# Moving one output store of the last row tile to the ScalarE queue

## Chip, cores, metric

The kernel runs on one core of one Trainium2 chip. The metric is device time in microseconds (us), the median of the runs of one kernel. Besides it the text uses the *span*, the time from the first to the last instruction in a profiled run, and the *tail*, the part of the span after the last VectorE copy has ended. Both are read from the trace, in nanoseconds (ns) where that matters.

## The reference, cut to what matters

Two linear-attention blocks A and B run on the same input `x` (2048 rows, 640 columns, bf16), and a gate for each row mixes their outputs:

```python
g = _sigmoid((x * gate_w).sum(-1, keepdims=True))
a = _A_ref(x, A_wqkv, A_wo)
b = _B_ref(x, B_wqkv, B_wo)
return g * a + (1 - g) * b          # 1 x 2048 x 640, bf16
```

Only the last step concerns us: the output leaves the core in 16 row tiles of 128 rows by 640 columns.

## The kernel before

The kernel lists its operations with their dependencies, and a small scheduler fixes the order on each engine before the program is built. The last row tile is computed in two column pieces, so that the first can be copied and stored while TensorE works on the second:

```python
def o_post(t, ps, lo, hi, eng):
    os_, bo = Buf("os", "os"), Buf("ob")
    w = hi - lo
    if eng == "ADD":
        ...                                     # tiles 0 to 12: add to an earlier partial sum
    elif eng == "DVE":
        op("DVE", lambda e: e.tensor_copy(OST[:, os_.slot, 0:w], psw(ps, w)), ...)
    else:
        op("ACT", lambda e: e.activation(OST[:, os_.slot, 0:w], psw(ps, w), ACT.Copy), ...)
    final.append(dma("SP", "out%d_%d" % (t, lo),
                     outd[128 * t : 128 * t + 128, lo:hi],
                     lambda: OST[:, os_.slot, 0:w], 128 * w * 2, ins=[os_], outs=[bo]))

def out_last(t):
    for lo, hi, eng in ((0, 512, "ACT"), (512, D, "DVE")):
        ps = Buf("o", "ps")
        for X in XS:
            o_mm(X, t, ps, lo, hi)
        o_post(t, ps, lo, hi, eng)
...
for o in final:
    nc.sync.wait_ge(o.sem, o.count)             # SyncE waits for every store to land
```

Below, the *large store* is that of columns 0 to 511 of the last tile (128 KB), the *small store* that of columns 512 to 639 (32 KB). Both are issued by SyncE ("SP").

## Time and profile before

| | before |
|---|---|
| time, median of 3 runs | 189.82 us (189.81 to 189.86) |
| span of the profiled run | 189.0 us |
| TensorE busy | 184.9 us, 98% |
| last matmul starts | 186.635 us |
| last VectorE copy ends | 187.254 us |
| tail | 1.751 us |

The page of the kernel before: the busy time of each engine, and the chain of waits followed back from the last instruction.

```profile
span 189.0 us, 3188 instructions
...
PE 184.9 (98%) x1246; PEld 108.3 (57%) x1270; DVE 128.6 (68%) x252; ACT 95.9 (51%) x172; POOL 0.3 (0%) x6
...
PE 96%; DMA 2%; issue 1%; SPq 0%; DVE 0%; DVEq 0%
```

TensorE (PE) is busy from end to end and makes up 96% of the chain. The store that is moved is issued after TensorE is done, so the tail is all that this change can touch.

The timeline of the tail, kernel before (start, duration, engine, line, operation; SPq is SyncE's list of DMA issues):

```profile
186.39 0.60 ACT L971 ACTIVATE TSB<-ps 128x512 bf16<-128x512 f32 x1 [1.46 <-PE ps L925]
186.96 0.29 DVE L969 CAST TSB<-ps 128x128 bf16<-128x128 f32 x1 [7.33 <-PE ps L925]
187.01 0.33 SPq L349 DMA_DIRECT2D out_dram<-TSB  x1
...
187.39 0.43 SPq L349 DMA_DIRECT2D out_dram<-TSB  x1
```

The small copy ends at 187.25, but SyncE issues the large store until 187.35 and takes up the small one only at 187.39. That wait is what the change wants to remove.

The DMA view of the last 4 us, kernel before. Each character is one slice of 0.1 us from 185.0 on: the busy share of the 16 DMA engines in tenths, and then what they moved.

```profile
DMA  0000000079996100000000000000399954820000
GB/s 0 0 0 0 0 0 0 13 256 371 384 371 218 26 0 0 0 0 0 0 0 0 0 0 0 0 0 0 123 338 338 338 164 95 192 52 0 0 0 0
...
q1 hardware_dynamic: 432, 0.33, 25.3%
...
out_dram<-TSB SPq DMA_DIRECT2D x1, 128.0 KB, 1.7
out_dram<-TSB SPq DMA_DIRECT2D x1, 32.0 KB, 1.6
```

The second burst, `399954820`, is the two stores: the large one fills the engines (`3999`), there is a dip (`54`), and the small one follows (`82`). Then comes 0.35 us in which no data moves and the landing is still awaited. From issue to landing the stores take 1.7 and 1.6 us, most of the tail.

### The profile page before, as it was taken

Reading aid. Unit: us, or ns where it says so; the run is one execution under the profiler, and the core shown is the slowest. Engines: PE = TensorE matmul, PEld = TensorE weight load, DVE = VectorE, ACT = ScalarE, POOL = GpSimd, SP = SyncE. Lnnn points to the kernel's source line nnn. Section 1 sums busy time; section 2 is a strip of 40 time slices with the busy share of each in tenths; the row PEclk is TensorE's granted clock in tenths of the full one; section 3 lists DMA queues with packets and bytes.
Section 4 is the critical chain, followed back from the end, with each engine's and each line's share of the span. In section 5 each row is a group of like instructions: output and inputs, shape, how many; then the busy total and the mean of one; then the engine's idle time right before and its main releaser. Section 6 shows DMA issues by size and latency. Waiting matters only on the chain.

```text
span 189.0 us, 3188 instructions
## 1 busy us (share of the span) xinstructions
PE 184.9 (98%) x1246; PEld 108.3 (57%) x1270; DVE 128.6 (68%) x252; ACT 95.9 (51%) x172; POOL 0.3 (0%) x6
## 2 busy tenths in 40 slices
PE   8999999999999999999999999999999999999995
PEld 3555555555565656656557556655666655555552
DVE  2389888888833556477787698888996962765600
ACT  3255565656554545544584777877626495100012
POOL 0000000000000000000000000000000000000000
PEclk9999999999999999999999999999999999999999
DMA  6999999996014011012000006340011055133322
GB/s 194 283 157 141 242 393 365 356 222 139 3 43 106 0 38 35 0 35 30 8 16 18 3 0 147 104 104 5 0 40 30 17 142 129 38 137 107 136 75 69
DMA packets 29469, 19.42 MB, mean 103 GB/s; under 512 B 17390, under 2 KB 29198, under 8 KB 29454
## 3 DMA queue, kind: packets, MB, share of 16 engines
q1 hardware_dynamic: 29300, 19.17, 39.4%
q8 instruction: 10, 0.16, 0.4%
q10 hardware_dynamic: 154, 0.05, 0.1%
q14 instruction: 5, 0.04, 0.1%
HBM read 9.95 MB, written 2.64 MB: 67 GB/s over the span
## 4 chain that ended last, share of the span: by engine, by line
PE 96%; DMA 2%; issue 1%; SPq 0%; DVE 0%; DVEq 0%
PE ps L925 23%; PE ps L755 22%; PE ps L632 18%; PE ps L502 18%; PE ps L503 5%; PE ps L633 5%; DMA XN<-in_A_x_dram 2%; PE ps L673 2%; PE ps L709 1%; SPq L349 0%; PE ps L449 0%; PE ps L710 0%; PE ps L838 0%; DVE TSB L969 0%; PE ps L483 0%
## 5 line engine op out<-in xcount | busy, mean ns | idle before, releaser
L502 PE MATMUL ps<-WKW,XT 128*128 128x512 bf16 x154 | 43.6, 384 | 0.1
L772 ACT ACTIVATE EK<-ps 128x512 bf16<-128x512 f32 x40 | 23.9, 599 | 31.3 <-PE ps L755 30.1
L503 PE MATMUL ps<-WKW,XT 128*128 128x128 bf16 (+1 forms) x160 | 35.3, 221 | 0.3
L535 ACT ACTIVATE EK<-ps 128x640 bf16<-128x640 f32 x32 | 22.3, 703 | 12.8 <-PE ps L503 8.6
L502 PEld LDWEIGHTS ps<-WKW,XT 128*128 128x128 bf16 x160 | 15.8, 99 | 19.1 <-DVE XT L464 0.6
L755 PE MATMUL ps<-XT,WQA 128*128 128x512 bf16 x96 | 24.0, 379 | 0.1
L755 PE MATMUL ps<-XT,WQB 128*128 128x512 bf16 x95 | 23.3, 379 | 0.4 <-issue 0.2
L632 PE MATMUL ps<-XN,PKB 128*128 128x512 bf16 x80 | 23.5, 379 | 0.0
L782 DVE TENSOR_SCALAR EK<-EK 128x512 bf16<-128x512 bf16 x40 | 11.6, 290 | 17.5 <-ACT EK L772 17.4
L632 PE MATMUL ps<-XN,PKA 128*128 128x512 bf16 x78 | 23.1, 379 | 0.1
L633 PE MATMUL ps<-XN,PKA 128*128 128x129 bf16 x80 | 17.6, 220 | 0.1
L633 PE MATMUL ps<-XN,PKB 128*128 128x129 bf16 x80 | 17.6, 220 | 0.0
L925 PE MATMUL ps<-WPA,EX 128*128 128x128 bf16 (+1 forms) x117 | 17.0, 297 | 0.2
L925 PE MATMUL ps<-WPB,PKA 128*128 128x128 bf16 (+1 forms) x117 | 16.1, 297 | 0.2
L503 PEld LDWEIGHTS ps<-WKW,XT 128*128 128x128 bf16 x160 | 15.8, 99 | 0.0
L755 PEld LDWEIGHTS ps<-XT,WQB 128*128 128x128 bf16 x100 | 10.9, 118 | 8.5 <-issue 0.2
L755 PEld LDWEIGHTS ps<-XT,WQA 128*128 128x128 bf16 x100 | 10.6, 117 | 8.1
L538 DVE TENSOR_SCALAR EK<-EK 128x640 bf16<-128x640 bf16 x32 | 10.4, 325 | 7.0 <-ACT EK L535 7.0
L632 PEld LDWEIGHTS ps<-XN,PKA 128*128 128x128 bf16 x80 | 9.4, 117 | 7.9
L632 PEld LDWEIGHTS ps<-XN,PKB 128*128 128x128 bf16 x80 | 9.4, 117 | 7.8
L971 ACT ACTIVATE TSB<-ps 128x640 bf16<-128x640 f32 (+1 forms) x3 | 2.0, 668 | 23.2 <-PE ps L925 23.2
L546 DVE SCALAR_TENSOR_TENSOR PKA<-ps,EK 128x640 bf16<-128x640 f32 x16 | 13.2, 825 | 0.6
(78 smaller groups left out, 233.1 us busy)
## 6 DMA issues: line engine op xcount, KB each, us to landing
out_dram<-TSB SPq DMA_DIRECT2D x15, 160.0 KB, 1.8
XN<-in_A_x_dram SPq DMA_DIRECT2D x1, 2240.0 KB, 8.8
WKW<-in_A_wqkv_dram SPq DMA_DIRECT2D x5, 160.0 KB, 3.4
WKW<-in_B_wqkv_dram SPq DMA_DIRECT2D x5, 160.0 KB, 4.1
WQA<-in_A_wqkv_dram SPq DMA_DIRECT2D x1, 800.0 KB, 10.5
WQB<-in_B_wqkv_dram SPq DMA_DIRECT2D x1, 800.0 KB, 11.7
WVA<-in_A_wqkv_dram SPq DMA_DIRECT2D x1, 800.0 KB, 12.8
WVB<-in_B_wqkv_dram SPq DMA_DIRECT2D x1, 800.0 KB, 14.1
```

The source lines that it names most:

```text
L502: e.matmul(a[:, 0:512], l, WK[X][:, c, 0:512], start=(c == 0), stop=(c == NC - 1))
L503: return e.matmul(a[:, 512:w], l, WK[X][:, c, 512:w], start=(c == 0), stop=(c == NC - 1))
L535: op("ACT", lambda e: e.activation(EK[:, ek.slot, :], psw(ps, D), ACT.Exp), act_cost(D), ins=[ps] + first, outs=[ek], name="ke")
L538: lambda e: e.tensor_scalar(EK[:, ek.slot, :], EK[:, ek.slot, :], 1.0, EPS, op0=ALU.min, op1=ALU.add),
L546: lambda e: e.scalar_tensor_tensor(PKt[X][:, t, :], psw(ps, D), 0.0, EK[:, ek.slot, :], op0=ALU.max, op1=ALU.add),
L632: e.matmul(a[:, 0:512], l, XN[:, t, 0:512], start=(t == 0), stop=(t == NT - 1))
L633: return e.matmul(a[:, 512 : D + 1], l, XN[:, t, 512 : D + 1], start=(t == 0), stop=(t == NT - 1))
L673: r = e.matmul(PS[0:GR, ps.slot, GR * i : GR * i + GR], WV[X][:, c, lo : lo + GR], gv[:, c, :, lo // 5 : lo // 5 + 24], start=(c == 0), st ...
L755: r = e.matmul(PS[:, ps.slot, :], WQ[X][:, c, g::5], XT[:, c, 512 * b : 512 * b + 512], start=(c == 0), stop=(c == NC - 1),)
L772: lambda e: e.activation(EQ[:, eq.slot, :], PS[:, ps.slot, :], ACT.Exp),
L782: lambda e: e.tensor_scalar(EQ[:, eq.slot, :], EQ[:, eq.slot, :], 1.0, EPS, op0=ALU.min, op1=ALU.add),
L925: r = e.matmul(a[:, l0 - lo : h0 - lo], PQ[X, b][:, g, 128 * (t % 4) : 128 * (t % 4) + 128], WP[X][:, g, l0:h0], start=(X == first and g = ...
```

## The change

The intent: give the small store an issuing engine that is idle. ScalarE has nothing to do after its copy ends at 186.99. (The diff also gives `o_post` a default, so that all other stores stay on SyncE.)

```diff
-    def o_post(t, ps, lo, hi, eng):
+    def o_post(t, ps, lo, hi, eng, q="SP"):
@@
         final.append(
             dma(
-                "SP",
+                q,
                 "out%d_%d" % (t, lo),
@@ out_last
-            o_post(t, ps, lo, hi, eng)
+            o_post(t, ps, lo, hi, eng, "ACT" if hi == D else "SP")
```

The built programs differ in one instruction: the small store is the last of ScalarE's list instead of the last of SyncE's.

## The prediction

> **What bounds the kernel now.** The span is 189.0 us; the page gives PE 184.9 us busy (98%), and the chain of waits is 96% PE. Only the tail is not PE, and the change touches only the tail. From the timeline (us from the span's start): the last matmul ends 186.87; the VectorE cast of the last 128 columns runs 186.96 to 187.25 and ScalarE's copy of the other 512 ends 186.99. SyncE then issues two stores of the last row tile: the 512-column one at 187.01 for 0.33 us, the 128-column one at 187.39 for 0.43 us. They land at 188.75 and 188.96 (issue to landing 1.73 and 1.57), SyncE passes its last wait, and the span ends at 189.0. So about 2.1 us follow the last matmul; most of that is the store's flight, which the change leaves alone.
>
> **What the change does.** The order of instructions on PE, VectorE and GpSimd is the same; one DMA issue moves from the end of SyncE's list to the end of ScalarE's, still waiting for the VectorE cast. Nothing else is added or removed: same bytes, same waits at the end on SyncE.
>
> **What it costs and saves.** Today the cast is ready at 187.25 but SyncE is busy with the other store until 187.35 and begins the second at 187.39. Stores that found SyncE idle began 0.03 us after the producer's end (13 VectorE cases in the timeline) and took 0.33 us; those issued right behind another took 0.43. ScalarE has been idle since 186.99, so its store should begin at 187.28 and be issued by 187.61, against 187.82: up to 0.21 us sooner, 0.11 from starting, 0.10 from the shorter issue.
>
> Not all of it arrives. Both stores use the same 16 DMA engines: the 512-column packets run from 187.84 to 188.38 today (about 48 ns each, 8 per engine), the 128-column ones from 188.33 to 188.60 (18 ns each). Coming 0.2 us earlier, the small packets interleave with the large, and the landing of the large store may slip a little. The Trainium skill, "DMA: Bandwidth & Descriptors", section "Issuing engines are not separate DMA queues", says just this: queues of different engines run on the same 16 DMA engines, and a second issuing engine saves only the sequencer's issue time. This trace agrees as far as it goes: at the start ScalarE's issue (0.12 to 0.47) overlapped SyncE's (0.00 to 0.39) with neither stretched. But that ScalarE load's first packet came 1.45 us after its issue, SyncE's after 1.01, against 0.83 for the 512-column store; if the second queue is slow to start again, the gain is lost or turns into a loss of some 0.3 us.
>
> All of the saving lies on the critical path, since nothing but this landing ends the kernel, until the 512-column store's landing at 188.75 takes over as the last. That caps the gain at about 0.2 us unless that store moves too. My estimate: 0.12 us off, 0.06%.
>
> **Prediction.** 189.70 us, 189.50 to 189.95 eight times in ten. Faster by over 2%: 0.005; within 2%: 0.99; slower by over 2%: 0.005.
>
> **What would show it.** The ScalarE queue issues its store near 187.28 for about 0.33 us; the 128-column packets begin near 188.1 on the second queue and mix with the 512-column ones; the two stores land within 0.1 us of each other near 188.8; the span shrinks by 0.1 to 0.2; everything before 187.0 stays the same within a few hundredths.
>
> **What would make it wrong.** Descriptor generation shared by the two queues, so that ScalarE's issue stretches to 0.43 or more; a slow first packet on the queue unused since the start; the large store slowed as much as the small one gains; or shifts of 0.1 us between runs that hide so small an effect.

## The result

| | before | changed |
|---|---|---|
| time, median (6 runs each) | 189.86 us (189.81 to 190.55) | 189.66 us (189.51 to 190.13) |
| ratio | | 0.9986, 95% interval 0.9969 to 1.0004 |
| span of the profiled run | 189.005 us | 188.787 us |
| last matmul starts | 186.635 | 186.450 |
| tail | 1.751 us | 1.721 us |

A ratio is the mean time of one kernel's fast runs over that of the other's of the same rounds, so it isn't quite the ratio of the medians. The interval contains 1. The span of the profiled run is 0.218 us shorter, but 0.185 of that was there already when the last matmul started, where the change has done nothing yet.

The page of the changed kernel:

```profile
span 188.8 us, 3188 instructions
...
PE 184.6 (98%) x1246; PEld 108.1 (57%) x1270; DVE 128.6 (68%) x252; ACT 95.9 (51%) x172; POOL 0.3 (0%) x6
...
PE 96%; DMA 2%; issue 1%; SPq 0%; DVE 0%; DVEq 0%
```

The timeline of its tail (ACTq is ScalarE's list of DMA issues):

```profile
186.21 0.60 ACT L971 ACTIVATE TSB<-ps 128x512 bf16<-128x512 f32 x1 [1.46 <-PE ps L925]
186.77 0.29 DVE L969 CAST TSB<-ps 128x128 bf16<-128x128 f32 x1 [7.33 <-PE ps L925]
186.83 0.33 SPq L349 DMA_DIRECT2D out_dram<-TSB  x1
...
187.10 0.36 ACTq L349 DMA_DIRECT2D out_dram<-TSB  x1
```

The mechanism works: the copy ends at 187.066, and the small store begins 0.032 us later instead of 0.136, and takes 0.363 us instead of 0.432. So its issue is over 0.173 us sooner after the copy. The tail shrank by only 0.030.

The DMA view of its last 4 us (slices of about 0.1 us from 184.9 on):

```profile
DMA  0000001699950000000000000007999950000000
GB/s 0 0 0 0 0 0 50 237 350 387 375 188 13 0 0 0 0 0 0 0 0 0 0 0 0 0 30 240 340 360 308 210 108 5 0 0 0 0 0 0
...
q1 hardware_dynamic: 288, 0.30, 21.1%
q10 hardware_dynamic: 144, 0.03, 3.9%
...
out_dram<-TSB SPq DMA_DIRECT2D x1, 128.0 KB, 1.7
out_dram<-TSB ACTq DMA_DIRECT2D x1, 32.0 KB, 1.6
```

The small store has a queue of its own (q10, 144 packets), and the dip is gone: the burst `799995` is solid. Between the two stores the DMA engines have no idle time left to give. The question is thus what held back 0.14 of the 0.17 us, and whether the time ratio of 0.9986 is an effect at all.

The small store step by step, in ns after the end of the last VectorE copy, from the records of the traces (the landing is that of the last of its 16 engines):

| | before | changed | gained |
|---|---|---|---|
| issue starts | 136 | 32 | 104 |
| issue takes | 432 | 363 | 69 |
| first packet | 1075 | 949 | |
| from end of issue to first packet | 507 | 554 | -47 |
| from first packet to end of last | 274 | 300 | -26 |
| from last packet to landing | 358 | 427 | -69 |
| from landing to end of span | 44 | 45 | -1 |
| tail | 1751 | 1721 | 30 |

The theory going into the experiments: the wait for SyncE was real, but behind it stood a second queue, the DMA engines busy with the large store. Rivals: a ScalarE queue that is slow because unused since the start; descriptor generation shared by both queues; and a real gain of 0.2 us somewhere else than in the tail.

### The profile page after: what moved, and what is told of

Same layout as the page of the kernel before. It is cut to its first block, busy times and chain, and to the rows that moved or that the text cites. A ratio compares the mean times of both kernels' runs of the same rounds, so it can differ in the third digit from the quotient of the medians.

```text
span 188.8 us, 3188 instructions
## 1 busy us (share of the span) xinstructions
PE 184.6 (98%) x1246; PEld 108.1 (57%) x1270; DVE 128.6 (68%) x252; ACT 95.9 (51%) x172; POOL 0.3 (0%) x6
## 4 chain that ended last, share of the span: by engine, by line
PE 96%; DMA 2%; issue 1%; SPq 0%; DVE 0%; DVEq 0%
PE ps L925 23%; PE ps L755 22%; PE ps L632 18%; PE ps L502 18%; PE ps L503 5%; PE ps L633 5%; DMA XN<-in_A_x_dram 2%; PE ps L673 2%; PE ps L709 1%; SPq L349 0%; PE ps L449 0%; PE ps L710 0%; PE ps L838 0%; DVE TSB L969 0%; PE ps L483 0%
```

## The experiments

Timed runs are compared with runs of the kernel before on the same chip. The tail is from one profiled run each; the two kernels that were profiled twice show how far it can be trusted. The four runs without timing (nolarge_sp, nolarge_act, tiny_act, warm_act): their granted clock was 1.00 like that of all the others, and only their tails are used. The runs come from three chips: before_again, after_again, both_act and swap from one, nolarge_sp, nolarge_act, tiny_act and halves_sp from a second, three_sp, three_act and warm_act from a third; for the first pair of runs the record names no chip. So some tails are compared across chips, and of these three chips the kernel before was profiled on the first alone. What repeats across them: warm_act, on the third chip, has the changed kernel's tail within 3 ns, and the step from SyncE to ScalarE with nothing in the way is 42 ns on the second chip and 41 on the third.

### before_again and after_again: what repeats

No edit: the two kernels once more, 5 rounds each.

> The kernel before, unchanged, against itself. Tail = from the end of the last VectorE cast to the end of the span: 1.75 us in the first profile of before, 1.72 in that of after. If the tail is steady, it reads 1.75 within 0.02 here too, and the time ratio lies within 0.9985 to 1.0015: then a time ratio of 0.9986 for the change is no more than the scatter of the rest of the kernel. Rival (the change gains 0.2 us outside the tail): the ratio here is 1.000 within 0.0005, so that 0.9986 stands out.

> The changed kernel again. Theory (the effect is only in the tail, 0.03 us): tail 1.72 within 0.02, ratio 0.9998 with an interval that includes 1. Rival (a real gain of 0.2 us, from elsewhere than the tail): ratio 0.9990 or below, interval clear of 1, and the last matmul earlier than in the kernel before run beside it.

| | before | before_again | changed | after_again |
|---|---|---|---|---|
| ratio to before | | 0.9985 (0.9947 to 1.0022) | 0.9986 (0.9969 to 1.0004) | 0.9985 (0.9946 to 1.0024) |
| last matmul starts, us | 186.635 | 185.911 | 186.450 | 185.957 |
| tail, us | 1.751 | 1.754 | 1.721 | 1.725 |

The kernel before against *itself* gave 0.9985. So 0.9986 for the change says nothing, and the rival of a gain outside the tail has lost its evidence: after_again's 0.9985 is as low as that rival wanted, but its interval isn't clear of 1. The traces speak against the rival too. From 8.7 us on, the 297 instructions of VectorE start 0.162 to 0.191 us earlier in the changed kernel than in the kernel before, 0.185 at 8.8 us and 0.187 at the last copy, so nothing was gained between the start and the tail. The tail repeats within 4 ns, so a difference of 30 ns there is real.

Where does the scatter come from? Set side by side, VectorE's instructions in before_again start 0.740 us earlier than in before at 8.8 us, and from there to the end the difference stays between 0.71 and 0.74 us in 293 of 297 instructions (the other four, near 160 us, show 0.82). At the last copy it is 0.726, so all that reaches the end arises in the first 9 us. TensorE's timeline there, kernel before:

```profile
5.02 0.63 PE L502 MATMUL ps<-WKW,XT 128*128 128x512 bf16 x1
5.44 0.31 PE L503 MATMUL ps<-WKW,XT 128*128 128x128 bf16 x1
5.55 0.61 PE L502 MATMUL ps<-WKW,XT 128*128 128x512 bf16 x1
5.98 0.24 PE L503 MATMUL ps<-WKW,XT 128*128 128x128 bf16 x1
6.05 0.38 PE L502 MATMUL ps<-WKW,XT 128*128 128x512 bf16 x1
```

The same in before_again:

```profile
3.42 0.47 PE L502 MATMUL ps<-WKW,XT 128*128 128x512 bf16 x1
3.73 0.22 PE L503 MATMUL ps<-WKW,XT 128*128 128x128 bf16 x1
...
4.76 0.39 PE L502 MATMUL ps<-WKW,XT 128*128 128x512 bf16 x1
```

The 512-wide matmul takes 0.61 to 0.63 us until 5.6 us in the one run, and 0.38 or 0.39 from 4.8 us on in the other: TensorE changes to its fast pace at different times. The Trainium skill, "TensorE: Matmul & The Clock Gate", section "Part 1: The HAM clock gate (the "warmup" mystery)", describes such a gate: TensorE starts at half its clock, and a window of about 3.4 us that doesn't reset when a kernel starts decides when it is released, so the moment varies from run to run. The traces agree with the picture: one 512-wide and one 128-wide matmul together start every 0.53 us before the change of pace and every 0.27 us after it, and the packed trace of the kernel before holds a record of the full clock that begins at 5.997 us, just there (that of the changed kernel begins at 5.543). Six of the 13 traces have such a record, each 184.32 us long, which is 54 times 3.413. The profile's clock column reads 1.00 throughout in both runs and doesn't show it.

### both_act and swap: which queue, or which place in it?

```diff
-            o_post(t, ps, lo, hi, eng, "ACT" if hi == D else "SP")
+            o_post(t, ps, lo, hi, eng, "ACT")                          # both_act
+            o_post(t, ps, lo, hi, eng, "SP" if hi == D else "ACT")     # swap
```

> Both stores of the last row tile on the ScalarE queue, the small one behind the large one. If what counts is that the small store finds an idle sequencer, and not which queue it is in, the small store begins 0.37 us after the large one and takes 0.43, and the tail is 1.75 to 1.80, as before or worse. If the ScalarE queue as such is better, the tail is 1.72 or less. If a queue that has been unused since the start is slow to wake, the large store's first packet comes later than 0.83 us after its issue and the tail is above 1.80.

> The large store on the ScalarE queue, the small one on SyncE's. If the part of the gain that went missing (0.05 us to the first packet, 0.07 from the last packet to the landing) comes from two stores sharing the DMA engines or the descriptor generation, the tail is as in the changed kernel, 1.72 within 0.02. If it comes from a ScalarE queue slow to start, the small store in the warm SyncE queue is rid of it: first packet 0.83 us after its issue, tail about 1.66, with the large store landing late instead.

In both_act the small store, behind the large one again, begins 0.175 us after the copy's end (0.407 after the large one's issue, against 0.37 expected) and takes 0.444; the tail is 1.804 us, longer than before the change, as the first of the three expectations had it. An issuing engine that is free is what helps, not ScalarE as such. But the marks of the third expectation, a queue slow to wake, are just met too: the tail is over 1.80, and the large store's first packet comes 0.866 us after its issue, against 0.827 from SyncE. This run doesn't tell the two apart; of the 0.039 us, 0.035 are the longer issue (0.367 against 0.332). nolarge_act and warm_act below test the third. The ratio was 0.9995 (0.9949 to 1.0040).

In swap the small store, now alone on SyncE, begins 0.027 us after the copy and takes 0.333, better than in the changed kernel. Yet the tail is 1.765 us, worse than the changed kernel's 1.721; the ratio was 0.9975 (0.9933 to 1.0018). Neither expectation fits. The traces show why: the large store, issued by ScalarE, starts its packets 0.040 us later than in the changed kernel (0.628 against 0.588 after the copy's end), ends them 0.042 later, and the small store's last packet (1.292 against 1.249) and landing (1.720 against 1.676) come later by the same 0.04. Again no packet of the small store begins (0.994) before the large store's first engine is through (0.988). The small store's end follows the large store's, not its own issue.

### nolarge_sp, nolarge_act, tiny_act: what the large store costs the small one

All three give a wrong result. The first two leave the large store out (from the kernel before, and from the changed one); the third is the changed kernel with the large store cut to 16 columns, with its 128 rows and its issue kept.

```diff
+        if (t, lo, hi) == (NT - 1, 0, 512):     # nolarge_sp, nolarge_act
+            return
         final.append(dma(...
```
```diff
+        dw = 16 if (t, w) == (NT - 1, 512) else w     # tiny_act
-                outd[128 * t : 128 * t + 128, lo:hi],
-                lambda: OST[:, os_.slot, 0:w],
+                outd[128 * t : 128 * t + 128, lo : lo + dw],
+                lambda: OST[:, os_.slot, 0:dw],
```

> Wrong result on purpose: the 512-column store of the last row tile is left out, the 128-column store stays in SyncE's queue. Nothing is in its way, so this is the floor of the small store: issue 0.03 us after the cast's end for 0.33 us, first packet 0.83 us after the issue. If sharing with the large store holds the small one up, the tail here falls to about 1.45 to 1.55 us (1.75 in the kernel before, 1.72 changed). If the wait for the sequencer is all that matters, 1.60 to 1.70.

> Wrong result on purpose: the 512-column store is left out, the small store is on the ScalarE queue. Against nolarge_sp this is the price of the ScalarE queue alone: 0.04 us if only its issue is longer (0.36 against 0.33) and its start 0.005 later; 0.1 us or more if a queue unused since the start must wake up.

> Wrong result on purpose: the changed kernel with the large store cut to 16 of its 512 columns, still 128 rows, on SyncE's queue. It needs as many descriptors and the same issue, but hardly any time on the DMA engines. If the small store is held up by the bytes of the large one (48 ns for each of 8 packets per engine), the tail falls to that of nolarge_act within 0.03. If it is held up by what does not depend on bytes (generating descriptors for both, landing one after the other), it stays near 1.68 to 1.72.

| ns after the copy's end | nolarge_sp | nolarge_act | tiny_act | changed |
|---|---|---|---|---|
| issue starts | 27 | 33 | 32 | 32 |
| issue takes | 333 | 362 | 362 | 363 |
| first packet | 856 | 894 | 895 | 949 |
| last packet ends | 1122 | 1164 | 1163 | 1249 |
| landing | 1508 | 1550 | 1521 | 1676 |
| tail | 1553 | 1595 | 1565 | 1721 |

The timeline of the tail of tiny_act:

```profile
186.24 0.29 DVE L970 CAST TSB<-ps 128x128 bf16<-128x128 f32 x1 [7.33 <-PE ps L925]
186.29 0.33 SPq L349 DMA_DIRECT2D out_dram<-TSB  x1
186.56 0.36 ACTq L349 DMA_DIRECT2D out_dram<-TSB  x1
```

Both stores are issued exactly as in the changed kernel, overlapping, but with 4 KB instead of 128 KB in the first. The small store's packets then run as if it were alone (895 and 1163 ns, against 894 and 1164), with 128 data packets in either store as in the changed kernel. So descriptor generation shared by the two queues doesn't hold it up; that rival falls. What holds it up are the large store's bytes: 0.156 us from tiny_act to the changed kernel.

The three runs also give the sizes of the terms:

- The large store ahead of it on SyncE cost the small one 1751 - 1553 = 198 ns. The change removes this way of being held up.
- The ScalarE queue costs 1595 - 1553 = 42 ns more than SyncE's: 6 in the start, 29 in the issue, the rest after it.
- With both stores in flight at once, the large one still costs 1721 - 1595 = 126 ns, now at the DMA engines and in the landing.
- 198 - 42 - 126 = 30 ns, the gain that was measured.

The sum comes out by construction, because all its terms are differences of the same four tails; it is no proof. What the runs add is the size of each term. The last one is 126 ns against nolarge_act and 156 against tiny_act, since these two differ by 30 ns in their landing (see the end). Nor do the terms act independently: warm_act, next, shortens the small store's issue by 19 ns and the tail doesn't follow.

### warm_act: is the ScalarE queue slow because it was asleep?

```diff
-        o_post(t, ps, 0, D, "ACT")
+        o_post(t, ps, 0, D, "ACT", "ACT" if t == NT - 2 else "SP")     # on top of the change
```

> The changed kernel with the store of the last row tile but one also on the ScalarE queue, some 2 us earlier, so that the queue has just been used. If the price of the ScalarE queue (issue 0.363 against 0.332, first packet 0.03 to 0.04 us later) is that of a queue unused since the start, the small store's issue falls to 0.33 and the tail to about 1.69. If it is ScalarE's own, issue 0.36 and tail 1.72 as in the changed kernel.

The earlier store on ScalarE took 0.362 us to issue, the small one after it 0.344 instead of 0.363. So part of the longer issue does go when the queue has just been used, but the tail is 1.724 us, as in the changed kernel (1.721 and 1.725): the small store then waits at the DMA engines all the same. The rival is no explanation of the missing gain. Whether a queue that has just been used would be quicker with no large store in the way was not run. One run without timing rounds (189.71 us).

### halves_sp: an edit that did not do what it should

To get the large store out of the way earlier, ScalarE and VectorE were to share its copy, with all stores on SyncE.

```diff
+        elif w == 512:
+            op("ACT", ... OST[:, os_.slot, 0:256], psw(ps, 256) ...)
+            op("DVE", ... OST[:, os_.slot, 256:512], psw(ps, 512)[:, 256:512] ...)
```

> Correct result: the copy of the 512 columns is shared by ScalarE and VectorE, 256 each, and all stores stay on SyncE, as in the kernel before. The large store should begin near 0.41 us before the cast's end instead of 0.24, and SyncE be free when the cast ends, so that the small store issues 0.03 after it, for 0.33. If what holds the small store up is the large one in front of it, the tail falls to 1.55 to 1.65, below the changed kernel's 1.72, without the ScalarE queue. If the landing of the small store has a floor of its own near 1.7, no gain. The time ratio will say nothing: before against itself gave 0.9985.

The kernel's helper orders two writers of one buffer on different engines, so VectorE's half ran *after* ScalarE's, as the timeline of halves_sp shows:

```profile
186.05 0.38 ACT L969 ACTIVATE TSB<-ps 128x256 bf16<-128x256 f32 x1 [1.46 <-PE ps L925]
186.07 0.44 PE L925 MATMUL ps<-WPB,GSA 128*128 128x128 bf16 x5
186.46 0.42 DVE L970 CAST TSB<-ps 128x256 bf16<-128x256 f32 x1 [7.17 <-ACT TSB L969]
186.80 0.28 DVE L972 CAST TSB<-ps 128x128 bf16<-128x128 f32 x1
```

The large store came later than before, and so did the small copy: from the last matmul to the end 2.614 us, against 2.370 in the kernel before, with a tail of 1.818 us. The ratio was 1.0051 (0.9988 to 1.0114). The run tells nothing of the question. A version without that order can't be run, because both engines would read one PSUM bank at once. The same aim needs different banks, which the next experiment uses.

### three_sp and three_act: take the bytes away, then make the change again

The last tile in three column pieces, each in its own PSUM bank. three_sp keeps every store on SyncE; three_act adds the change.

```diff
-        for lo, hi, eng in ((0, 512, "ACT"), (512, D, "DVE")):
+        for lo, hi, eng in ((0, 256, "DVE"), (256, 512, "ACT"), (512, D, "DVE")):
```

> Correct result: the last row tile in three pieces of 256, 256 and 128 columns, all stored from SyncE. The middle piece's copy on ScalarE takes 0.38 us instead of 0.60, so its store starts near 0.45 us before the end of the last cast, carries half the bytes, and SyncE is free when the cast ends. If the bytes and the issue in front of the small store are all that hold it up, the tail falls to 1.55 to 1.60 us (floor without any large store: 1.553; changed kernel: 1.72), still on the SyncE queue, and the span to the last matmul grows by no more than 0.1. If landing on another store's heels costs as such, 1.65 or more.

> The change on top of three_sp: its last store on the ScalarE queue. With SyncE free the change has nothing left to save, so only the price of the ScalarE queue is left: a tail 0.03 to 0.05 us longer than three_sp's (nolarge_act against nolarge_sp: 0.042). If the ScalarE queue is better for another reason, the tail is no longer than three_sp's.

The timeline of the tail of three_sp:

```profile
188.15 0.33 SPq L349 DMA_DIRECT2D out_dram<-TSB  x1
188.31 0.29 DVE L969 CAST TSB<-ps 128x128 bf16<-128x128 f32 x1 [1.23 <-PE ps L925]
188.63 0.33 SPq L349 DMA_DIRECT2D out_dram<-TSB  x1
```

Timeline and issues of three_act (the first line of the issues is the 256-column store):

```profile
185.35 1.37 SPq L349 DMA_DIRECT2D out_dram<-TSB  x2
186.55 0.29 DVE L969 CAST TSB<-ps 128x128 bf16<-128x128 f32 x1 [1.22 <-PE ps L925]
186.88 0.36 ACTq L349 DMA_DIRECT2D out_dram<-TSB  x1
...
out_dram<-TSB SPq DMA_DIRECT2D x1, 64.0 KB, 1.5
out_dram<-TSB ACTq DMA_DIRECT2D x1, 32.0 KB, 1.5
```

| | before | changed | three_sp | three_act |
|---|---|---|---|---|
| small store's issue starts, takes, ns | 136, 432 | 32, 363 | 28, 332 | 33, 363 |
| first packet, ns | 1075 | 949 | 857 | 893 |
| tail, us | 1.751 | 1.721 | 1.510 | 1.551 |
| from the last 640-wide VectorE add to the end, us | 10.193 | 10.162 | 9.976 | 10.017 |

The last row counts the whole of the last three tiles, so it includes what the extra matmuls of three_sp cost. Before_again and after_again read 10.194 and 10.165 there. With the middle piece issued 0.45 us before the copy's end and half as many bytes, the small store meets an idle SyncE and idle DMA engines, and three_sp is 0.22 us shorter than the kernel before and 0.19 shorter than the changed one. That the middle store is smaller and that it comes earlier was not told apart. The tail, 1.510 us, missed the expected 1.55 to 1.60 on the low side: it is below even that of the lone store of nolarge_sp (1.553), which was therefore no floor. The last packet ends at 1.116 us, as there (1.122), but the landing follows after 0.349 us and not 0.386. And on top of it the change is a *loss* of 0.041 us, the same 0.042 that the lone stores showed as the price of the ScalarE queue. Of all versions here three_sp has the shortest tail, and its result is correct.

Its timed ratio was 0.9949 (0.9900 to 0.9999). That can't be the effect, which is 0.1% of the time: the runs of before beside it went from 189.81 to 192.21 us. The fastest runs, 189.60 against 189.81, differ by 0.21. Its profiled run had a late start (span 190.1 us, the 512-wide matmuls slow until 8.6 us), which is why only differences within the run are used. three_act: 0.9979 (0.9918 to 1.0041).

## Why the prediction was right, and where it was off

- **Time: right.** 189.70 was forecast and 189.66 measured, inside the range; "within 2%" was given 0.99. But the closeness of 0.04 us is luck, since the kernel before against itself differed by 0.15%.
- **The bound: right.** The chain is 96% TensorE, and from 9 us on everything but the tail was unchanged.
- **Start of the issue: right.** 0.03 us after the copy was forecast, 0.032 measured.
- **Length of the issue: off by 0.03.** "issued by 187.61", that is 0.33 us, as on an idle SyncE; ScalarE took 0.363. So 0.17 us were gained there and not 0.21.
- **The size of the gain: off.** "My estimate: 0.12 us off"; the tail shows 0.030. The term that was mis-sized is the sharing of the DMA engines. The text said that the small packets "interleave with the large" and left 0.09 us for it (0.21 less 0.12). Of the 0.173 us that the issue gained, 0.143 were lost after it: 47 ns up to the first packet, 26 among the packets, 69 up to the landing. The large store's bytes account for 126 to 156 ns of tail (nolarge_act and tiny_act). That "the landing of the large store may slip a little" was right: 1.504 us after the copy instead of 1.494. The small store doesn't overtake: no packet of it began (949 ns) before the large store's first engine was through (its first semaphore packet at 943 ns), and swap shows the same (994 and 988). The Trainium skill, "DMA: Bandwidth & Descriptors", section "Queues, rings and completion order", says that an engine drains a whole packet of several descriptors from one queue before it turns to another. That fits the order seen here, though no run tells how packets were formed.
- **"the two stores land within 0.1 us of each other near 188.8": off.** They land 0.172 us apart (1.504 and 1.676 after the copy), and 0.173 in swap.
- **"everything before 187.0 stays the same within a few hundredths": wrong.** It moved by 0.185 us, through TensorE's varying start. The doubt "shifts of 0.1 us between runs that hide so small an effect" was right and too small.
- **Doubts that didn't come true.** Shared descriptor generation (tiny_act) explains none of the missing gain, and a sleeping queue (warm_act) 19 ns of the issue but none of the tail; the loss of 0.3 us didn't come. The prediction's own sign that two issues don't stretch each other was weak, since SyncE's first issue took 0.39 us and its idle ones 0.33; tiny_act is the better one.

What stays open: of the 156 ns between tiny_act and the changed kernel, 86 arise up to the end of the last packet and 69 between it and the landing, which takes 427 ns in the changed kernel and 428 in swap, but 358 in the kernel before and in tiny_act. In the changed kernel the 32 landing records of the two stores follow one another without a gap over 395 ns, about 12.7 each, so that the small store's come right behind the large one's. Within one store the 16 landing records come in nearly even steps although its packets end unevenly: 13.3 ns in the lone stores, mostly 11.7 in a small store behind another, mostly 10 in the last store of three_sp. That fits landings that queue up one by one, but whether they do, or each waits for the large store's writes, no run here tells apart. Nor is it known why the lone stores of nolarge_sp and nolarge_act take 386 ns for that, 28 more than tiny_act's; 19 of the 28 lie in the pace of the records (200 ns for the 16 against 181).

## What to carry to other kernels

Moving an issue to an idle engine removes only the wait for the issuing engine; ask next which queue stands behind it, here the DMA engines full of the neighbouring store's bytes. At the end of a kernel, make the store *ahead* of the last one smaller and earlier (0.22 us here for both together) before looking for another queue (0.03 us, and a loss of 0.04 once the way is clear). And for effects of a tenth of a per cent, run the kernel against itself first, then compare a stretch of the traces that starts after the scatter.

## What the Trainium skill lacked or had wrong

- "DMA: Bandwidth & Descriptors", "Issuing engines are not separate DMA queues", says that issuing from several engines saves only the issue time. That held as an upper bound: 173 ns of issue were saved and 30 ns arrived. It lacks that the two issuing engines differ: with nothing in the way, ScalarE took 0.362 us to issue the small store and SyncE 0.333, and the tail was 42 ns longer from ScalarE.
- The same page, "Latency and other measured facts", gives about 600 ns to the first byte without saying from where it counts. Here the first packet came 0.829 us after the start of an undisturbed SyncE issue (0.496 after its end) and 0.861 after ScalarE's.
- The same page doesn't say that an issue right behind another takes longer: 0.43 us, against 0.33 on an idle SyncE.
- No page was found to give the time from the last data packet to the landing when two stores finish together: 0.43 us here, against 0.34 to 0.39 for stores that finish alone.
- "TensorE: Matmul & The Clock Gate", "Part 1", lets the change to full clock vary by about half a microsecond from run to run; further on, the same part reports 6, 11 or 14 slow matmuls for one kernel, which is a wider spread. Here the last slow 512-wide matmul began at 2.1 us in some traces, at 5.6 in another and at 8.1 in a third, and the start of the last matmul moved by 2.08 us between the earliest and the latest trace (185.909 in tiny_act, 187.985 in three_sp, whose extra matmuls are a small part of that).
